# Attention scores in row halves: two heads at once on TensorE, in a kernel of pooled attention followed by a gated two-layer product

## The chip, the cores and the metric

The kernel runs on one core of one Trainium2 chip. The metric is the device time of one execution in microseconds (us); 1000 ns are 1 us. All comparisons of times below use runs of the fast state. Even at full clock two executions of one kernel can differ by over a microsecond (the kernel before took from 305.03 to 306.49 us within one set of rounds, both with a clock of 1.0), so wherever a few hundred nanoseconds matter I read them from the profile, not from the difference of two times.

## The reference, cut to what matters

Eight batches of eight heads, 576 queries, head width 64. Keys and values are first averaged over groups of eight rows, so each head has only 72 keys. Then follow plain attention, and on its output a product, `h * cos(h)`, and a second product.

```python
k_p = k.reshape(B, H, Sp, pool, D).mean(axis=3)       # Sp = 72
v_p = v.reshape(B, H, Sp, pool, D).mean(axis=3)
scores = scale * np.matmul(q, k_p.transpose(0, 1, 3, 2))
...                                                     # softmax, attn @ v_p
h = x @ w_in                                            # 4608 x 512 by 512 x 2048
g = h * np.cos(h)
return g @ w_out                                        # 2048 x 512
```

## The kernel before

The tokens are worked off in nine tiles of 512. Each tile has an up projection (64 matmuls of 512 columns) and a down projection (64 more). Attention for the batch that comes next is slipped between the down matmuls, at fixed places, so that TensorE never runs dry. PSUM is the memory, divided into banks, into which the matmuls write their results. A "unit" is four heads by 256 queries; the "remainder" is all eight heads by the last 64 queries.

```python
def scores(b, u, pair):                       # pair: two PSUM banks
    (c0, n), (h0, nh) = u
    flat = pair.rearrange("p a n -> p (a n)")
    for i in range(nh):
        pj, hp = divmod(h0 + i, 2)
        g, r = divmod(ROW * pj + ORDER[c0 // 64], 2)
        nc.tensor.matmul(flat[:Sp, i * n:(i + 1) * n]...,
                         lhsT=kz[b % 2][:, 2 * (h0 + i) + r, 0:Sp],     # 128 rows, one half zero
                         rhs=att["qT", b][:, g:g + n // 64, hp * 64:hp * 64 + 64])
    ...                                       # one exponential on ScalarE for the unit
...
# places in a tile's down projection: (before which down matmul, what)
fill = [(1, scores of the remainder), (12, its values)]
fill[1:1] = [(5, S_(0, 0))]                   # S_(unit, bank pair): scores; V_: values
fill += [(15, S_(1, 2)), (18, V_(0, 0)), (25, S_(2, 2)), (28, V_(1, 1)), (35, S_(3, 2)), (38, V_(2, 0)),
         (46, V_(3, 1))]
```

(The first `fill` line is shortened.) A score sums over 64 numbers, half of the array's 128 rows. The transposed queries of a head lie in the upper or the lower 64 rows, depending on `r`. The kernel before always runs all 128 rows and pads the keys with zeros in the half that doesn't count.

The softmax here doesn't subtract the row's maximum and nothing guards it: scores larger than these inputs give would overflow.

Of the kernel before, what the change touches and what calls it, by code (L numbers as in the profile page):

```python
# [10 lines left out]
BF16 = mybir.dt.bfloat16  # L11
ACTF = mybir.ActivationFunctionType
ADD = mybir.AluOpType.add

POOL = 8
# [4 lines left out]
def kernel(  # L20
# [9 lines left out]
    nc = tc.nc  # L30
    B, H, S, D = q.shape
    Sp = S // POOL
# [3 lines left out]
    scale = 1.0 / math.sqrt(D)  # L36
# [17 lines left out]
    wpool = ctx.enter_context(tc.tile_pool(name="wpool", bufs=1))  # L54
# [9 lines left out]
    g_sb = wpool.tile([128, FFCH, TILE], BF16, name="g_sb")  # L64

    SpA = -(-Sp // 16) * 16
    kz = [wpool.tile([128, 2 * H, SpA], BF16, name=f"kz{i}") for i in range(2)]

    kpz = [wpool.tile([SpA, H, 4, D], BF16, name=f"kpz{i}") for i in range(2)]

    vz = [wpool.tile([Sp, KCH, 4, D], BF16, name=f"vz{i}") for i in range(2)]

# [6 lines left out]
    staged = {}  # L79

    def even_view(src, b, j0=0, j1=KCH):
        return src[b, 2 * j0:2 * j1].rearrange("(j a) (p t) d -> (a p) j (t d)", a=2, t=ROW)

    def load_even(dst, b, src, j0=0, j1=KCH):
        nc.gpsimd.dma_start(out=dst[:, j0:j1].rearrange("p j t d -> p j (t d)"), in_=even_view(src, b, j0, j1))  # L85
# [37 lines left out]
    att = {}  # L123
    half = (slice(0, 64), slice(64, 128))

    def v_part(b):
        return vz[b % 2][:, :, 0:4:3, :]

    def put_kz(b, ps, pj0, pj1, copy):
        dst = kz[b % 2].rearrange("p (j a r) n -> p j a r n", a=2, r=2)  # L130
        for a in range(2):
            for r in range(2):
                copy(out=dst[half[r], pj0:pj1, a, r, 0:Sp], in_=ps[half[a]])

    def pool_add(b, which):

        st = staged.pop((which, b))
        x = st[:, 0]
        s = st[:, 1].rearrange("p h t d -> p (h t d)").bitcast(FP32).rearrange(
            "p (h t d) -> p h t d", h=H, t=POOL // 2)  # L140
        add = nc.gpsimd.tensor_tensor
        add(out=s, in0=x[:, :, 0:4, :], in1=x[:, :, 4:8, :], op=ADD)  # L142
        add(out=s[:, :, 0:2, :], in0=s[:, :, 0:2, :], in1=s[:, :, 2:4, :], op=ADD)  # L143
        if which == "k":
            for slot in (0, 3):
                add(out=kpz[b % 2][:Sp, :, slot, :], in0=s[:, :, 0, :], in1=s[:, :, 1, :], op=ADD)  # L146
        else:
            s = s.rearrange("p (j a) t d -> p j a t d", a=2)
            add(out=v_part(b), in0=s[..., 0, :], in1=s[..., 1, :], op=ADD)

    def pool_k_mm(b, bank, pj0, pj1):

        kb = staged["k", b]
        ps = bank[:, 0:(pj1 - pj0) * Sp].rearrange("p (j n) -> p j n", n=Sp)
        for pj in range(pj0, pj1):
            for t in range(ROW):
                for rows in half:
                    nc.tensor.matmul(ps[rows, pj - pj0, :], lhsT=kb[rows, pj, t, :], rhs=groups[rows, t, :],
                                     start=(t == 0), stop=(t == ROW - 1))
        return lambda copy: put_kz(b, ps, pj0, pj1, copy)  # L160

    def pool_v_mm(b, pair):
        vb = staged["v", b]
# [5 lines left out]
                              in_=pair[:Sp, :, 0:KCH * D].rearrange("p a (j d) -> p a j d", j=KCH))  # L169

    def k_transpose(b):
        nc.sync.dma_start_transpose(out=kz[b % 2], in_=kpz[b % 2].rearrange("p h s d -> p (h s d)"))


    QB = KCH * ROW // 2
# [11 lines left out]
    def q_transpose_mm(b, bank, g0, g1):  # L187
# [5 lines left out]
            nc.tensor.matmul(ps[:, g - g0, :], q_flat(b)[:, g * 128:(g + 1) * 128], identity, is_transpose=True)  # L193
        return lambda copy: copy(out=att["qT", b][:, g0:g1, :], in_=ps)  # L194

    def scores(b, u, pair):
        (c0, n), (h0, nh) = u
        flat = pair.rearrange("p a n -> p (a n)")
        for i in range(nh):
            pj, hp = divmod(h0 + i, 2)  # L200
            g, r = divmod(ROW * pj + ORDER[c0 // 64], 2)
            nc.tensor.matmul(flat[:Sp, i * n:(i + 1) * n].rearrange("p (g n) -> p g n", n=64),  # L202
                             lhsT=kz[b % 2][:, 2 * (h0 + i) + r, 0:Sp],
                             rhs=att["qT", b][:, g:g + n // 64, hp * 64:hp * 64 + 64])
        ex = asb.tile([Sp, 4 * 256], BF16, name="ex", tag="ex", bufs=EX)
        nc.scalar.activation(out=ex[:, 0:nh * n], in_=flat[:Sp, 0:nh * n], func=ACTF.Exp, scale=scale / POOL)  # L206
        att["ex", b, u] = ex

    def x_out(b, u, rows):
        (c0, n), (h0, nh) = u  # L210
        return xT[rows, h0 // 2:(h0 + nh) // 2, b * S + c0:b * S + c0 + n]

    def cols(x, u):
        n = u[0][1]
        return x[:, 0:n * u[1][1] // 2].rearrange("p (j n) -> p j n", n=n)

    def inverse_tile(w):
        lnc = asb.tile([128, 512], FP32, name="lnc", tag="lnc", bufs=1)
        inv = asb.tile([128, 512], FP32, name="inv", tag="inv", bufs=3)
        return lnc[:, 0:w], inv[:, 0:w]  # L220

    def values(b, u, pair, later=None):

        (c0, n), (h0, nh) = u
        ex = att.pop(("ex", b, u))
        for i in range(nh):
            pj, hp = divmod(h0 + i, 2)
            nc.tensor.matmul(pair[:, hp, (i // 2) * n:(i // 2 + 1) * n],  # L228
                             lhsT=vz[b % 2][:, pj, 2 * hp:2 * hp + 2, :].rearrange("p a d -> p (a d)"),
                             rhs=ex[:, i * n:(i + 1) * n])  # L230
        w = nh * n // 2
        lnc, inv = inverse_tile(w)
        for hp in range(2):
            nc.scalar.activation(out=lnc[half[1 - hp]], in_=pair[half[1 - hp], hp, 0:w], func=ACTF.Ln)  # L234
        nc.scalar.activation(out=inv, in_=lnc, func=ACTF.Exp, scale=-1.0)  # L235

        def mul():
            for hp in range(2):
                nc.vector.tensor_mul(out=x_out(b, u, half[hp]), in0=cols(pair[half[hp], hp, :], u),  # L239
                                     in1=cols(inv[half[1 - hp]], u))  # L240

        if later is None:
            mul()
        else:
            later.append(mul)

    def sums_first(b, u, cs):

        (c0, n), (h0, nh) = u
        ex = att["ex", b, u]  # L250
        for i in range(nh):
            hp = i % 2
            nc.tensor.matmul(cs[hp * 64:hp * 64 + 64, (i // 2) * n:(i // 2 + 1) * n], lhsT=ones[:Sp, :],
                             rhs=ex[:, i * n:(i + 1) * n])
        w = nh * n // 2
        lnc, inv = inverse_tile(w)
        nc.scalar.activation(out=lnc, in_=cs[:, 0:w], func=ACTF.Ln)
        nc.scalar.activation(out=inv, in_=lnc, func=ACTF.Exp, scale=-1.0)
        att["inv", b, u] = inv

    def values_then(b, u, ao):

        (c0, n), (h0, nh) = u
        ex = att.pop(("ex", b, u))
        for i in range(nh):
            pj, hp = divmod(h0 + i, 2)
            nc.tensor.matmul(ao[hp * 64:hp * 64 + 64, (i // 2) * n:(i // 2 + 1) * n],
                             lhsT=vz[b % 2][:, pj, 3 * hp, :], rhs=ex[:, i * n:(i + 1) * n])
        nc.vector.tensor_mul(out=x_out(b, u, slice(0, 128)), in0=cols(ao, u), in1=cols(att.pop(("inv", b, u)), u))

    def exp_tables():
        nc.scalar.preload_act_table_set("natural_log_exp_and_others")  # L272
# [49 lines left out]
    warm = consts.tile([128, 512], BF16, name="warm")  # L322
    nc.vector.memset(warm, 1.0)
    exp_tables()
    nc.vector.memset(kz[0], 0.0)

    kv_even_tiles(0)
    q_tile(0)
# [1 line left out]
    nc.sync.dma_start(out=k_first.rearrange("p (j n) -> p j n", j=2), in_=even_view(k, 0, 0, 2))  # L330
    nc.scalar.copy(out=staged["k", 0][:, 0:2].rearrange("p j t d -> p (j t d)"), in_=k_first)
    load_even(staged["q", 0], 0, q, 0, 2)

    row_of = consts.tile([128, ROW], FP32, name="row_of")
    for rows in half:
# [2 lines left out]
    first_of = consts.tile([128, Sp], FP32, name="first_of")  # L338
    nc.gpsimd.iota(first_of, pattern=[[POOL, Sp]], base=0, channel_multiplier=0,
                   allow_small_or_imprecise_dtypes=True)  # L340
    load_even(staged["k", 0], 0, k, 2, 4)
    identity = consts.tile([128, 128], BF16, name="identity")
    make_identity(nc, identity)
    load_even(staged["q", 0], 0, q, 2, 4)
    load_even(staged["v", 0], 0, v)
    dist = consts.tile([128, ROW, Sp], FP32, name="dist")
    sign = consts.tile([128, ROW, Sp], FP32, name="sign")
    groups = consts.tile([128, ROW, Sp], BF16, name="groups")
# [1 line left out]
                            in1=first_of.unsqueeze(1).to_broadcast([128, ROW, Sp]), op=mybir.AluOpType.subtract)  # L350
# [6 lines left out]
    gate = consts.tile([1, 1], BF16, name="gate")  # L357
# [11 lines left out]
    load_w_out(0)  # L369
    load_even(staged["v", 1], 1, v)  # L370
    for i in range(2):
        nc.gpsimd.memset(kpz[i], 0.0)  # L372
    for cg in range(1, 4):
        load_w_out(cg)

# [22 lines left out]
    sums_first(0, us[1], obanks[1])  # L398
    scores(0, us[2], banks[0])
    scores(0, us[3], banks[2])  # L400
    nc.vector.memset(kz[1], 0.0)
    nc.vector.memset(vz[1], float(POOL))
    pool_v_mm(0, banks[1])
    sums_first(0, us[2], obanks[0])
# [9 lines left out]
    for t in range(NT):  # L414
        b = t + 1
# [29 lines left out]
        def V_(n, bank, wait=None):  # L445
            return lambda: values(b, us[n], banks[bank], wait)
# [25 lines left out]
            sin_tables()  # L472
        if 0 < t and b + 1 < B:

            nc.gpsimd.tensor_copy(out=gate, in_=kz[b % 2][0:1, 0, 0:1])  # L475
        if b + 1 < B:
            load_kv(b + 1, "k", k)
            load_q(b + 1)
# [32 lines left out]
```

## Time and profile before

| | before |
|---|---|
| time, median of all 6 runs beside the change | 305.52 us (305.22 to 306.61) |
| span in the profile | 303.6 us |
| TensorE busy | 97% |
| one steady tile (start of an up projection to the next) | 31.65 us |

In the views PE stands for TensorE's matmuls and PEld for its weight loads, ACT for ScalarE, DVE for VectorE, POOL for GpSimd. The chain in order of time (start, length, what) goes on after the score unit at 68.89 us with seven down matmuls:

```profile
69.32 1.51 PE obank L297 x7
```

The groups of instructions split by shape say (line, engine, operation, names, shapes, count; then busy us and mean ns of one; then idle time of that engine just before, and what ended it):

```profile
L202 PE MATMUL bank<-qT,kz 128*72 128x256 bf16 x128 | 19.2, 273 | 0.3 <-ACT qT L194 0.2
L202 PE MATMUL bank<-qT,kz 128*72 128x64 bf16 x64 | 3.5, 198 | 0.0
...
L297 PEld LDWEIGHTS <-g_sb 128*128 128x128 bf16 x560 | 53.8, 98 | 50.5 <-issue 0.2
```

The mean of 273 ns is the length of one record, not its cost: successive ones start 109 ns apart. And the weight loads run ahead. The load for the first score of the unit at 68.72 us starts at 68.51:

```profile
68.51 0.11 PEld L202 LDWEIGHTS <-kz 128*72 128x72 bf16 x1
```

The idle time of the weight loads before the down matmuls is 50.5 us, some 90 ns a load. Only 0.2 us of it is put down to "issue", because the view names a cause for the longer gaps alone.

### The profile page before, as it was taken

Reading aid. Unit: us, or ns where it says so; the run is one execution under the profiler, and the core shown is the slowest. Engines: PE = TensorE matmul, PEld = TensorE weight load, DVE = VectorE, ACT = ScalarE, POOL = GpSimd, SP = SyncE. Lnnn points to the kernel's source line nnn. Section 1 sums busy time; section 2 is a strip of 40 time slices with the busy share of each in tenths; the row PEclk is TensorE's granted clock in tenths of the full one; section 3 lists DMA queues with packets and bytes.
Section 4 is the critical chain, followed back from the end, with each engine's and each line's share of the span. In section 5 each row is a group of like instructions: output and inputs, shape, how many; then the busy total and the mean of one; then the engine's idle time right before and its main releaser. Section 6 shows DMA issues by size and latency. Waiting matters only on the chain.

```text
span 303.6 us, 4590 instructions
## 1 busy us (share of the span) xinstructions
PE 295.3 (97%) x1798; PEld 152.5 (50%) x1798; DVE 173.3 (57%) x213; ACT 206.6 (68%) x255; POOL 131.8 (43%) x92
## 2 busy tenths in 40 slices
PE   6899999999999999999999999999999999999995
PEld 2645654446544554455445544565455544444444
DVE  7558546574566555745575566637574657425712
ACT  3886897469956995689668966797569946605500
POOL 8573017985963596339823990399100000000000
PEclk9999999999999999999999999999999999999999
DMA  7999999649455934694379527871911120031032
GB/s 145 193 207 206 209 203 196 147 82 177 101 129 103 171 74 100 123 170 86 85 146 162 105 48 178 125 145 35 167 26 36 37 69 0 21 85 35 0 71 71
DMA packets 47846, 33.90 MB, mean 112 GB/s; under 512 B 25936, under 2 KB 43088, under 8 KB 47824
## 3 DMA queue, kind: packets, MB, share of 16 engines
q0 software_dynamic: 19744, 18.07, 38.0%
q1 hardware_dynamic: 27920, 15.41, 22.0%
q8 instruction: 14, 0.23, 0.3%
q10 hardware_dynamic: 160, 0.13, 0.2%
q14 instruction: 8, 0.07, 0.1%
HBM read 36.70 MB, written 9.44 MB: 152 GB/s over the span
## 4 chain that ended last, share of the span: by engine, by line
PE 85%; DMA 9%; POOL 3%; ACT 1%; issue 0%; DVE 0%; POOLq 0%; ACTq 0%
PE obank L297 38%; PE bank L284 36%; DMA w_out_sb<-in_moe_w_out_dram 6%; PE bank L228 5%; PE bank L202 4%; DMA w_in_sb<-in_moe_w_in_dram 3%; PE bank L315 1%; POOL kpz L372 1%; POOL kv_st L85 1%; POOL q_b L85 1%; ACT L272 0%; ACT cos L291 0%; POOL identity masks.py:199 0%; ACT ex L206 0%; DVE o_sb L303 0%
## 5 line engine op out<-in xcount | busy, mean ns | idle before, releaser
L297 PE MATMUL obank<-w_out_sb,g_sb 128*128 128x512 bf16 x560 | 134.2, 379 | 0.1
L284 PE MATMUL bank<-xT,w_in_sb 128*128 128x512 bf16 x576 | 126.3, 379 | 0.0
L291 ACT ACTIVATE cos<-bank,half_pi 128x1024 f32<-128x1024 f32 x72 | 80.1, 1114 | 67.3 <-PE bank L284 67.3
L294 DVE TENSOR_TENSOR g_sb<-bank,cos 128x1024 bf16<-128x1024 f32 x72 | 88.1, 1225 | 50.1 <-ACT cos L291 50.1
L284 PEld LDWEIGHTS <-w_in_sb 128*128 128x128 bf16 x576 | 56.1, 98 | 67.3 <-issue 0.4
L297 PEld LDWEIGHTS <-g_sb 128*128 128x128 bf16 x560 | 53.8, 98 | 50.5 <-issue 0.2
L239 DVE TENSOR_TENSOR xT<-bank,inv 64x512 bf16<-64x512 f32 (+1 forms) x72 | 45.3, 629 | 49.5 <-ACT inv L235 49.0
L142 POOL TENSOR_TENSOR kv_st<-kv_st 72x2048 f32<-72x2048 bf16 x12 | 48.8, 4064 | 34.7 <-DMA kv_st<-in_k_dram 34.7
L234 ACT ACTIVATE lnc<-bank 64x512 f32<-64x512 f32 (+1 forms) x72 | 39.2, 544 | 4.7 <-PE bank L228 3.1
L206 ACT ACTIVATE ex<-bank 72x1024 bf16<-72x1024 f32 (+1 forms) x40 | 36.1, 925 | 0.7 <-PE bank L202 0.6
L303 DVE COPY o_sb<-obank 128x512 f32<-128x512 f32 x35 | 23.6, 690 | 16.7 <-PE obank L297 16.1
L143 POOL TENSOR_TENSOR kv_st<-kv_st 72x1024 f32<-72x1024 f32 x12 | 28.2, 2349 | 1.0
L202 PE MATMUL bank<-qT,kz 128*72 128x256 bf16 (+1 forms) x192 | 22.7, 248 | 0.3 <-ACT qT L194 0.2
L202 PEld LDWEIGHTS <-kz 128*72 128x72 bf16 x192 | 17.5, 114 | 9.1 <-issue 0.6
L235 ACT ACTIVATE inv<-lnc 128x512 f32<-128x512 f32 (+1 forms) x36 | 21.0, 583 | 1.1
L228 PE MATMUL bank<-ex,vz 72*128 72x256 bf16 (+1 forms) x176 | 20.1, 243 | 0.3 <-ACT ex L206 0.2
L228 PEld LDWEIGHTS <-vz 72*128 72x128 bf16 x176 | 13.7, 97 | 9.9 <-issue 0.7
L146 POOL TENSOR_TENSOR kpz<-kv_st 72x512 bf16<-72x512 f32 x12 | 15.0, 1267 | 0.5
L272 ACT ACT_TABLE_LOAD x9 | 11.5, 1283 | 0.9 <-PEq L495 0.7
L475 POOL COPY gate<-kz 1x1 bf16<-1x1 bf16 x5 | 0.9, 180 | 25.9 <-DMA kz<-kpz 25.9
L275 ACT ACT_TABLE_LOAD x9 | 11.5, 1283 | 0.2
L85 POOL DMA_DIRECT2D q_b<-in_q_dram x10 | 7.7, 773 | 2.9 <-DMA w_in_sb<-in_moe_w_in_dram 1.4
(57 smaller groups left out, 91.1 us busy)
## 6 DMA issues: line engine op xcount, KB each, us to landing
out_dram<-o_sb SPq DMA_DIRECT2D x70, 128.0 KB, 2.4
kv_st<-in_v_dram POOLq DMA_DIRECT2D x8, 576.0 KB, 12.8
kv_st<-in_k_dram POOLq DMA_DIRECT2D x7, 576.0 KB, 7.7
q_b<-in_q_dram POOLq DMA_DIRECT2D x6, 576.0 KB, 9.8
w_in_sb<-in_moe_w_in_dram POOLq DMA_DIRECT2D x4, 512.0 KB, 13.0
w_out_sb<-in_moe_w_out_dram POOLq DMA_DIRECT2D x4, 512.0 KB, 18.6
q_b<-in_q_dram POOLq DMA_DIRECT2D x4, 288.0 KB, 11.5
g_sb<-in_k_dram SPq DMA_DIRECT2D x1, 576.0 KB, 3.4
```

Of the source, the lines that this page charges most:

```text
L142: add(out=s, in0=x[:, :, 0:4, :], in1=x[:, :, 4:8, :], op=ADD)
L143: add(out=s[:, :, 0:2, :], in0=s[:, :, 0:2, :], in1=s[:, :, 2:4, :], op=ADD)
L202: nc.tensor.matmul(flat[:Sp, i * n:(i + 1) * n].rearrange("p (g n) -> p g n", n=64), lhsT=kz[b % 2][:, 2 * (h0 + i) + r, 0:Sp], rhs=att["q ...
L206: nc.scalar.activation(out=ex[:, 0:nh * n], in_=flat[:Sp, 0:nh * n], func=ACTF.Exp, scale=scale / POOL)
L228: nc.tensor.matmul(pair[:, hp, (i // 2) * n:(i // 2 + 1) * n], lhsT=vz[b % 2][:, pj, 2 * hp:2 * hp + 2, :].rearrange("p a d -> p (a d)"), ...
L234: nc.scalar.activation(out=lnc[half[1 - hp]], in_=pair[half[1 - hp], hp, 0:w], func=ACTF.Ln)
L239: nc.vector.tensor_mul(out=x_out(b, u, half[hp]), in0=cols(pair[half[hp], hp, :], u), in1=cols(inv[half[1 - hp]], u))
L284: nc.tensor.matmul(h[:, j, :], lhsT=w_in_sb[fc // 4][:, ki, (fc % 4) * 128:(fc % 4 + 1) * 128], rhs=xT[:, ki, t * TILE:(t + 1) * TILE], st ...
L291: nc.scalar.activation(out=cos, in_=h, func=ACTF.Sin, bias=half_pi[:, :1])
L294: nc.vector.tensor_mul(out=g_sb[:, 2 * fp:2 * fp + 2, :], in0=h, in1=cos)
L297: nc.tensor.matmul(o, lhsT=g_sb[:, fc, ms * 128:(ms + 1) * 128], rhs=w_out_sb[fc // 4][:, fc % 4, :], start=(fc == 0), stop=(fc == FFCH - 1))
L303: nc.vector.tensor_copy(out=o[:, 0:n], in_=ps)
```

## The change

The intent: two heads whose queries lie in different row halves run at the same time, each in its half of the array and with a PSUM bank of its own. The keys are kept once in each half, without zeros. On the side, the loads of batch 0 are issued sooner, and the identity for the transposes is built behind them.

```diff
-    kz = [wpool.tile([128, 2 * H, SpA], BF16, name=f"kz{i}") for i in range(2)]
-    kpz = [wpool.tile([SpA, H, 4, D], BF16, name=f"kpz{i}") for i in range(2)]
+    kk = [wpool.tile([128, H, SpA], BF16, name=f"kk{i}") for i in range(2)]
+    kp2 = [wpool.tile([SpA, H, 2, D], BF16, name=f"kp2{i}") for i in range(2)]
...
+        for i in [i + 2 * a for k in range(0, nh, 4) for i in (k, k + 1) for a in range(2)]:
+            bank, c = divmod(ex_col(u, i), nh * n // 2)
...
-                             lhsT=kz[b % 2][:, 2 * (h0 + i) + r, 0:Sp],
-                             rhs=att["qT", b][:, g:g + n // 64, hp * 64:hp * 64 + 64])
+                             lhsT=kk[b % 2][half[r], h0 + i, 0:Sp],
+                             rhs=att["qT", b][half[r], g:g + n // 64, hp * 64:hp * 64 + 64])
...
     load_even(staged["q", 0], 0, q, 0, 2)
+    load_even(staged["k", 0], 0, k, 2, 4)
...                                            (index ramps)
-    load_even(staged["k", 0], 0, k, 2, 4)
+    load_even(staged["q", 0], 0, q, 2, 4)
+    load_even(staged["v", 0], 0, v)
     identity = consts.tile([128, 128], BF16, name="identity")
     make_identity(nc, identity)
-    load_even(staged["q", 0], 0, q, 2, 4)
-    load_even(staged["v", 0], 0, v)
```

(Cut: the zeroing of `kz`, the copies into `kk`, and the index `ex_col`, by which the values find a head's columns in their new order. Heads 0, 2, 1, 3 of a unit now follow each other.)

More of the change, by code (lines that the diff above doesn't have):

```diff
@@ L127, in v_part, with put_kk @@
         return vz[b % 2][:, :, 0:4:3, :]
-    def put_kz(b, ps, pj0, pj1, copy):
-        dst = kz[b % 2].rearrange("p (j a r) n -> p j a r n", a=2, r=2)
+    def put_kk(b, ps, pj0, pj1, copy):
+        dst = kk[b % 2].rearrange("p (j a) n -> p j a n", a=2)
         for a in range(2):
             for r in range(2):
-                copy(out=dst[half[r], pj0:pj1, a, r, 0:Sp], in_=ps[half[a]])
+                copy(out=dst[half[r], pj0:pj1, a, 0:Sp], in_=ps[half[a]])
     def pool_add(b, which):
@@ L144, in pool_add @@
         if which == "k":
-            for slot in (0, 3):
-                add(out=kpz[b % 2][:Sp, :, slot, :], in0=s[:, :, 0, :], in1=s[:, :, 1, :], op=ADD)
+            for slot in range(2):
+                add(out=kp2[b % 2][:Sp, :, slot, :], in0=s[:, :, 0, :], in1=s[:, :, 1, :], op=ADD)
         else:
@@ L159, in pool_k_mm @@
                                      start=(t == 0), stop=(t == ROW - 1))
-        return lambda copy: put_kz(b, ps, pj0, pj1, copy)
+        return lambda copy: put_kk(b, ps, pj0, pj1, copy)
     def pool_v_mm(b, pair):
@@ L171, in k_transpose @@
     def k_transpose(b):
-        nc.sync.dma_start_transpose(out=kz[b % 2], in_=kpz[b % 2].rearrange("p h s d -> p (h s d)"))
+        nc.sync.dma_start_transpose(out=kk[b % 2], in_=kp2[b % 2].rearrange("p h s d -> p (h s d)"))
     QB = KCH * ROW // 2
@@ L194, in q_transpose_mm, with ex_col @@
         return lambda copy: copy(out=att["qT", b][:, g0:g1, :], in_=ps)
+    def ex_col(u, i):
+        (c0, n), (h0, nh) = u
+        return (i // 2 % 2 * (nh // 2) + i // 4 * 2 + i % 2) * n
     def scores(b, u, pair):
         (c0, n), (h0, nh) = u
-        flat = pair.rearrange("p a n -> p (a n)")
-        for i in range(nh):
+        for i in [i + 2 * a for k in range(0, nh, 4) for i in (k, k + 1) for a in range(2)]:
+            bank, c = divmod(ex_col(u, i), nh * n // 2)
             pj, hp = divmod(h0 + i, 2)
             g, r = divmod(ROW * pj + ORDER[c0 // 64], 2)
-            nc.tensor.matmul(flat[:Sp, i * n:(i + 1) * n].rearrange("p (g n) -> p g n", n=64),
-                             lhsT=kz[b % 2][:, 2 * (h0 + i) + r, 0:Sp],
-                             rhs=att["qT", b][:, g:g + n // 64, hp * 64:hp * 64 + 64])
+            nc.tensor.matmul(pair[:Sp, bank, c:c + n].rearrange("p (g n) -> p g n", n=64),
+                             lhsT=kk[b % 2][half[r], h0 + i, 0:Sp],
+                             rhs=att["qT", b][half[r], g:g + n // 64, hp * 64:hp * 64 + 64])
         ex = asb.tile([Sp, 4 * 256], BF16, name="ex", tag="ex", bufs=EX)
-        nc.scalar.activation(out=ex[:, 0:nh * n], in_=flat[:Sp, 0:nh * n], func=ACTF.Exp, scale=scale / POOL)
+        nc.scalar.activation(out=ex[:, 0:nh * n].rearrange("p (a n) -> p a n", a=2), in_=pair[:Sp, :, 0:nh * n // 2],
+                             func=ACTF.Exp, scale=scale / POOL)
         att["ex", b, u] = ex
@@ L229, in values @@
                              lhsT=vz[b % 2][:, pj, 2 * hp:2 * hp + 2, :].rearrange("p a d -> p (a d)"),
-                             rhs=ex[:, i * n:(i + 1) * n])
+                             rhs=ex[:, ex_col(u, i):ex_col(u, i) + n])
         w = nh * n // 2
@@ L253, in sums_first @@
             nc.tensor.matmul(cs[hp * 64:hp * 64 + 64, (i // 2) * n:(i // 2 + 1) * n], lhsT=ones[:Sp, :],
-                             rhs=ex[:, i * n:(i + 1) * n])
+                             rhs=ex[:, ex_col(u, i):ex_col(u, i) + n])
         w = nh * n // 2
@@ L267, in values_then @@
             nc.tensor.matmul(ao[hp * 64:hp * 64 + 64, (i // 2) * n:(i // 2 + 1) * n],
-                             lhsT=vz[b % 2][:, pj, 3 * hp, :], rhs=ex[:, i * n:(i + 1) * n])
+                             lhsT=vz[b % 2][:, pj, 3 * hp, :], rhs=ex[:, ex_col(u, i):ex_col(u, i) + n])
         nc.vector.tensor_mul(out=x_out(b, u, slice(0, 128)), in0=cols(ao, u), in1=cols(att.pop(("inv", b, u)), u))
@@ L324 @@
     exp_tables()
-    nc.vector.memset(kz[0], 0.0)
     kv_even_tiles(0)
@@ L371 @@
     for i in range(2):
-        nc.gpsimd.memset(kpz[i], 0.0)
+        nc.gpsimd.memset(kp2[i], 0.0)
     for cg in range(1, 4):
@@ L400 @@
     scores(0, us[3], banks[2])
-    nc.vector.memset(kz[1], 0.0)
     nc.vector.memset(vz[1], float(POOL))
@@ L473 @@
         if 0 < t and b + 1 < B:
-            nc.gpsimd.tensor_copy(out=gate, in_=kz[b % 2][0:1, 0, 0:1])
+            nc.gpsimd.tensor_copy(out=gate, in_=kk[b % 2][0:1, 0, 0:1])
         if b + 1 < B:
```

## The prediction

> **What bounds the kernel now.** I read the engine shares first, then the chain of waits in order of time, then the groups split by shape, and last narrow windows of the timeline around single matmuls.
>
> The first view is the page's busy times and its chain. TensorE is busy for 97% of the span and carries 85% of the chain; no other engine comes near.
>
> ```profile
> PE 295.3 (97%) x1798; PEld 152.5 (50%) x1798; DVE 173.3 (57%) x213; ACT 206.6 (68%) x255; POOL 131.8 (43%) x92
> ...
> PE 85%; DMA 9%; POOL 3%; ACT 1%; issue 0%; DVE 0%; POOLq 0%; ACTq 0%
> ```
>
> The chain in order of time (start, length, what) says where this holds. Up to 38.10 us it is the queue of loads, of which the second quarter of the down weights lands last; TensorE stands in it without a break for six tiles, and one detour through ScalarE comes in the eighth:
>
> ```profile
> 6.14 10.26 DMA w_in_sb<-in_moe_w_in_dram
> ...
> 20.92 17.18 DMA w_out_sb<-in_moe_w_out_dram
> 38.10 0.04 issue
> 38.14 0.81 PE obank L297 x3
> 38.95 0.44 PE bank L202 x4
> ...
> 67.53 0.22 PE obank L297
> 67.75 0.27 PE bank L202 x8
> 68.02 0.86 PE obank L297 x4
> 68.89 0.44 PE bank L202 x4
> ...
> 257.45 1.11 ACT cos L291
> 258.56 0.02 issue
> 258.58 1.28 ACT L272
> 259.87 0.01 ACTq L234
> 259.87 0.01 issue
> 259.88 0.60 ACT ex L206
> 260.48 0.04 issue
> 260.52 0.39 PE bank L228 x8
> ```
>
> So between 48.5 and 257.4 us every nanosecond added to or taken from TensorE's stream shows in the end time; outside that stretch there are waits that swallow it. The score matmuls are line 202. A unit of four heads by 256 queries costs 0.44 us of stream, and the remainder unit (eight heads by 64 queries) 0.27 us. There are 32 units and 8 remainders (128 matmuls and 64 in the groups split by shape), so the scores hold 32 x 0.437 + 8 x 0.273 = 16.2 us of TensorE. If two heads at a time were free of cost, at most half of it, some 8 us or 2.6%, could go.
>
> **What the Trainium skill says.** Three places bear on this. "TensorE: Matmul & The Clock Gate", section "Part 3: Packing small matmuls", says that matmuls in different row groups run at the same time and start about 4 ns apart. The trace agrees: pooling V already works in 64-row halves with a bank each (line 166), its two matmuls start 3 to 4 ns apart, and a pair of 256 columns follows the next at 106 to 109 ns, where line 202 takes 109 ns for a single one. "TensorEngine Tiling (Array Packing)", section "Gotcha 1: PSUM Pressure", says that different row tiles cannot use one PSUM bank at once; the change gives each half its own bank, as line 166 does. The same page, section "Key Properties", says "Mode switching requires drain: Changing tiling mode (not just tile) drains the TensorE", without a figure. This kernel shows the figure, and it decides the case.
>
> **What a switch costs.** Two narrow windows of the timeline, each cut so that it starts with the last matmul before a switch (start, length, line, shapes, count):
>
> ```profile
> 13.55 0.27 PE L202 MATMUL bank<-qT,kz 128*72 128x256 bf16 x1
> 13.75 0.30 PE L166 MATMUL bank<-kv_st,groups 64*72 64x256 bf16 x2
> ...
> 37.40 0.27 PE L166 MATMUL bank<-kv_st,groups 64*72 64x256 bf16 x1
> 37.61 0.26 PE L228 MATMUL bank<-ex,vz 72*128 72x64 bf16 x3
> ```
>
> In both, start to start is 0.20 us (203 and 202 ns in the records), where two matmuls of one mode would be 109 ns apart. Going into row halves costs 94 ns, coming out 93 ns; nothing else was being waited for, and the weight loads, which normally run ahead, start only at the end of the gap too. The up projection into pooling K (26.08 to 26.39, 309 instead of 216 ns) and back (27.55 to 27.68, 127 instead of about 32) gives +93 and +95. Two small costs go with it: the second pair after a switch comes after 136 ns instead of 109, and the second matmul after coming back is 11 ns late (227 instead of 216).
>
> **The change part by part.**
>
> A unit of four heads in the down projection. Before: 4 x 109 = 437 ns. After: in 94, first pair to second pair 136, its second half 4, then last score to next down matmul 202 (109 of stream and 93 out), 11 for the late second one: 447 ns. The halved streaming is spent on the two switches: +10 ns a unit.
>
> A remainder unit, eight matmuls of 64 columns. Before 8 x 35 = 273 ns with the edges. These were bound not by columns but by the 72-column weight loads, at 35 ns each. Line 158 (pooling K, 72 columns in both halves) shows pairs of such size: 53 ns from first to second pair, then 33. After: in 94, then 53 + 35 + 35 for four pairs, 3 for the second half of the last, 35 of stream, 93 out, 11 late: 359 ns, +86 ns.
>
> In the six tiles where TensorE is never idle, each has one remainder and four units: 86 + 4 x 10 = 126 ns, six times is 0.76 us. These lie fully on the path.
>
> The eighth tile: its remainder is followed by a wait of 407 ns before the values at 260.52 (ScalarE ends the last cosine, loads its table, does the exponential). 86 ns more TensorE work before it disappears in it: 0.
>
> The first tile: before the values of its remainder are followed by the down matmuls of the second weight quarter, TensorE is 292 ns late because those weights land at 38.098; later a wait of 200 ns at 47.5 stands before values, behind a ScalarE that is nearly always busy. The 86 and 4 x 10 ns fall into these: 0 to 0.04.
>
> Batch 0, before 17.6 us: two runs of eight scores become four pairs each, 0.87 to about 0.45 us of stream. The switch out of the second run also disappears, since pooling V is in the same mode. But ScalarE is busy back to back here from 9.41 to 19.67 us, and the scores wait for transposed queries which ScalarE copies at 12.39 to 12.96. I expect 0.2 to 0.3 us sooner for TensorE at 17.6 us, and this ends in a longer wait for the weights at 38.1: 0.
>
> The zeroing of the padded keys on VectorE (2 x 0.59 us) was beside other work: 0. The zeroed GpSimd tile becomes half as large, 2 x 1.8 us to about 2 x 0.9 us. After it comes the issue of the down weights at 20.92; they land 17.2 us later, because the queue in front of them is full. Each load lands 2.5 to 2.8 us behind its predecessor. An earlier issue brings nothing. The transposes of keys by DMA halve too (3.6 us each, issued about ten microseconds before use): 0.
>
> The moved loads. The pieces of K, Q and V of batch 0 are issued 0.6 to 1.2 us sooner, since the identity (0.22 + 0.89 us) goes behind them; the weights keep their place. Before, the second and third pieces landed 1.53 and 1.68 us after their predecessor, while an equal piece in the full queue took 1.43 (24.34 to 25.77). If this slack of 0.10 + 0.25 us closes, everything behind lands up to 0.35 us sooner, the down weights included: 0 to -0.35, I take -0.15. On the other side the index ramps on GpSimd come about 0.8 us later, so the pooling matrix is ready at about 5.8 us instead of 5.1 and the first pooling matmul starts 0.4 us later. What follows waits for the Q load at 7.6 us, so 0 to 0.2 us is left of that, and the 9.4 to 19.7 stretch decides it: 0 to +0.1.
>
> Sum: +0.76 + 0.02 - 0.15 + 0.03 = +0.66, hence 305.33 + 0.6, about 305.9 us.
>
> **The rivals.** First: the switches are hidden, because weight loads of another row group are pulled ahead. Then 28 units would gain about 0.19 us and the remainders 0.1, about 6 us: 299 us, faster by 2%. For it: half of the score streaming really goes. Against it: the trace holds this very pair of neighbours, full rows into halves and back, at 94 and 93 ns each time. Second: a switch costs more between score and down matmuls than where I read it, for instance because the down weights then can't be loaded ahead of a 512-column matmul. At 50 ns more for each of 2 x 35 switches it is +3.5 us, 309. Against: the switch out of the up projection is the same size. Third: the start becomes the bound, that is, the late pooling matrix delays the first exponential by up to 0.4 us and ScalarE hands this on to 20 us. It would be hidden by the 292 ns wait at 38.1 except for some 0.1 us: 306.0. Fourth: the order of loads gains the whole 0.35 us and nothing else changes: 305.7.
>
> **Range and chances.** The on-path sum is two numbers of nearly equal size subtracted, so it is small whichever way the remainder comes out: 304.8 to 307.0 should hold it 8 times in 10; the upper side is longer because one of the three runs before was 306.61. Faster by over 2% needs the first rival in full (4%), slower by over 2% a switch of twice the size (2%).
>
> **What would show it.** In the changed profile a score unit in the steady tiles should show two pairs, each 3 to 4 ns apart, with 0.31 us from the down matmul before to the first score (216 + 94) and 0.20 us from the last score to the next down matmul; unit and remainder should hold 0.44 and 0.36 us of stream and a steady tile 31.77 us instead of 31.65. The load of the second down weights should land between 37.7 and 38.1, with TensorE waiting for it. I am wrong if the gaps at the switches are much under 90 ns (then faster), or if the stretch from 48.5 to 257.4 us changes by more than 1.5 us either way.

## The result, and the profile after

| | before | after |
|---|---|---|
| time, median of 6 | 305.52 us | 306.32 us (306.01 to 306.97) |
| span in the profile | 303.6 us | 304.2 us |
| start of the second tile | 53.56 us | 53.48 us |
| one steady tile | 31.647 us | 31.768 us |
| eighth tile | 28.54 us | 28.54 us |
| from the start of the ninth tile to the end | 31.58 us | 31.58 us |

The ratio is 1.0024, with a 95% interval of 1.0006 to 1.0043. Ratios and intervals here are worked out from the fast runs of the same rounds, so not quite the ratio of the medians. The kernel is a little slower, and well within 2%. The tile rows come from the starts of the matmuls in the trace. The six steady tiles took 189.88 us before and 190.61 after: +0.73 us. The start gave back 0.08, and the two last tiles nothing: 0.65 us in sum, the difference of the unrounded spans (303.56 and 304.21).

The page's busy times and chain after:

```profile
PE 295.6 (97%) x1798; PEld 140.2 (46%) x1798; DVE 172.0 (57%) x211; ACT 206.4 (68%) x255; POOL 129.5 (43%) x92
...
PE 84%; DMA 11%; POOL 2%; ACT 1%; issue 0%; DVE 0%; POOLq 0%; ACTq 0%
```

TensorE is as busy as before, though its scores were to take half the time. The groups split by shape say why this line cannot show it:

```profile
L303 PEld LDWEIGHTS <-g_sb 128*128 128x128 bf16 x560 | 51.3, 98 | 56.2 <-issue 6.0
...
L207 PE MATMUL bank<-qT,kk 64*72 64x256 bf16 x128 | 13.0, 282 | 1.3 <-DVE qT L193 0.6 <-ACT qT L193 0.5
L207 PEld LDWEIGHTS <-kk 64*72 64x72 bf16 x192 | 6.6, 109 | 17.2 <-issue 16.8 <-DVE qT L193 0.4
L207 PE MATMUL bank<-qT,kk 64*72 64x64 bf16 x64 | 2.6, 201 | 0.0
```

The scores' busy time fell from 19.2 to 13.0 us and from 3.5 to 2.6, a handsome 7.1 us. What it was paid with stands in the other column: the weight loads' idle time rose from 9.1 to 17.2 us before the scores and from 50.5 to 56.2 before the down matmuls. (The "issue" part rose more, from 0.6 to 16.8 and from 0.2 to 6.0, but only because gaps that were too short to be named are now long enough.) In that time no weights are loaded ahead:

```profile
68.83 0.11 PEld L207 LDWEIGHTS <-kk 64*72 64x72 bf16 x2 [0.42 <-issue]
```

The first load of the new mode starts 308 ns after the start of the last down matmul (68.52 us), so 92 ns after the 216 ns of that one's stream. In the kernel before it started within 2 ns of the same matmul's start.

The chain in order of time, at the same place of the second tile as before:

```profile
40.66 0.04 issue
40.70 0.59 PE obank L303 x2
...
68.90 0.34 PE bank L207 x4
69.24 1.62 PE obank L303 x7
```

A reader who compares the score line alone sees 0.34 us instead of 0.44 and calls it a gain. But the seven down matmuls after it have grown from 1.51 to 1.62 us. The sum is 1.95 us before and 1.96 after: the chain books the switch back to full rows on the line that follows it. The first rows show the start: TensorE now waits at 40.7 us, for the third quarter of the down weights, where it waited at 38.1 for the second.

Two narrow windows of the timeline, each from the last matmul before a switch:

```profile
68.52 0.38 PE L303 MATMUL obank<-w_out_sb,g_sb 128*128 128x512 bf16 x1
68.83 0.30 PE L207 MATMUL bank<-qT,kk 64*72 64x256 bf16 x2
...
68.97 0.27 PE L207 MATMUL bank<-qT,kk 64*72 64x256 bf16 x1
69.17 0.39 PE L303 MATMUL obank<-w_out_sb,g_sb 128*128 128x512 bf16 x1
```

From start to start it is 309 ns into the halves, of which 216 are the stream of a down matmul, so 93 are lost; coming out it is 202, of which 109 are stream, so 93 again. The two scores of a pair start 4 ns apart, the second pair 137 ns after the first, and the second down matmul after the visit is 10 to 11 ns late.

### The profile page after: what moved, and what is told of

Same layout as the page of the kernel before. It is cut to its first block, busy times and chain, and to the rows that moved or that the text cites. A ratio compares the mean times of both kernels' runs of the same rounds, so it can differ in the third digit from the quotient of the medians.

```text
span 304.2 us, 4587 instructions
## 1 busy us (share of the span) xinstructions
PE 295.6 (97%) x1798; PEld 140.2 (46%) x1798; DVE 172.0 (57%) x211; ACT 206.4 (68%) x255; POOL 129.5 (43%) x92
## 4 chain that ended last, share of the span: by engine, by line
PE 84%; DMA 11%; POOL 2%; ACT 1%; issue 0%; DVE 0%; POOLq 0%; ACTq 0%
PE obank L303 39%; PE bank L290 36%; DMA w_out_sb<-in_moe_w_out_dram 6%; DMA w_in_sb<-in_moe_w_in_dram 5%; PE bank L234 5%; PE bank L207 3%; PE bank L321 1%; POOL q_b L84 1%; POOL kv_st L84 0%; POOL w_in_sb L112 0%; ACT L278 0%; ACT cos L297 0%; ACT ex L211 0%; DVE o_sb L309 0%; POOL row_of L342 0%
## 5 line engine op out<-in xcount | busy, mean ns | idle before, releaser
L303 PEld LDWEIGHTS <-g_sb 128*128 128x128 bf16 x560 | 51.3, 98 | 56.2 <-issue 6.0
L240 ACT ACTIVATE lnc<-bank 64x512 f32<-64x512 f32 (+1 forms) x72 | 39.1, 544 | 5.9 <-PE bank L234 4.7
L207 PE MATMUL bank<-qT,kk 64*72 64x256 bf16 (+1 forms) x192 | 15.6, 255 | 1.3 <-DVE qT L193 0.6
L145 POOL TENSOR_TENSOR kp<-kv_st 72x512 bf16<-72x512 f32 x12 | 14.9, 1263 | 0.5
L207 PEld LDWEIGHTS <-kk 64*72 64x72 bf16 x192 | 6.6, 109 | 17.2 <-issue 16.8
L479 POOL COPY gate<-kk 1x1 bf16<-1x1 bf16 x5 | 0.9, 180 | 25.9 <-DMA kk<-kp 25.9
```

What stands on the lines that cost most here:

```text
L207: nc.tensor.matmul(pair[:Sp, bank, c:c + n].rearrange("p (g n) -> p g n", n=64), lhsT=kk[b % 2][half[r], h0 + i, 0:Sp], rhs=att["qT", b][h ...
L240: nc.scalar.activation(out=lnc[half[1 - hp]], in_=pair[half[1 - hp], hp, 0:w], func=ACTF.Ln)
L303: nc.tensor.matmul(o, lhsT=g_sb[:, fc, ms * 128:(ms + 1) * 128], rhs=w_out_sb[fc // 4][:, fc % 4, :], start=(fc == 0), stop=(fc == FFCH - 1))
```

## The experiments

Theory: a visit to the row halves (one group of scores between down matmuls) has a fixed price, whatever is done in it. A unit of two pairs just about pays it and a remainder doesn't, so six steady tiles lose 0.73 us. Rivals: the reordered start costs the time; the pairs are concurrent only in appearance; the wait lies elsewhere, in the schedule or on ScalarE. Twelve kernels ran, all with correct results. "Tile" is the mean of the six steady tiles in the run's profile. Kernels that ran together share the runs of the kernel before: its median was 305.46 us beside the first four, 305.64 beside the next four, 305.41 beside the next three and 305.46 beside the last.

**The scores alone** (`scores_only`): the change without its moved loads.

```diff
     load_even(staged["q", 0], 0, q, 0, 2)
-    load_even(staged["k", 0], 0, k, 2, 4)
...
+    load_even(staged["k", 0], 0, k, 2, 4)
+    identity = consts.tile([128, 128], BF16, name="identity")
+    make_identity(nc, identity)
     load_even(staged["q", 0], 0, q, 2, 4)
     load_even(staged["v", 0], 0, v)
-    identity = consts.tile([128, 128], BF16, name="identity")
-    make_identity(nc, identity)
```

> The change without its moved loads and identity. Theory (fixed cost per visit to the row halves): a steady tile takes 31.77 us as in the changed kernel against 31.65 before, so +0.7 us in six tiles; the second quarter of the down weights lands at 38.1 us as before (38.098), not at 37.5, and TensorE waits for that one and not for the third. Time about 306.3 us, 0.7 to 0.8 over before. Rival (the start, reordered, is what costs): a steady tile may be as it is, but the time is that of before, 305.5, because the reordering is missing.

Measured: tile 31.769 us; median 306.41 us, ratio 1.0047 (1.0005 to 1.0089). Two of its six runs had a lowered clock (0.982) and over 310 us; one of them widens the interval. The four at full clock took 305.94 to 306.53. The second quarter of the down weights landed at 38.18 us, as before. The loss in the tiles is the same as in the whole change, so it comes from the scores.

**The loads alone** (`loads_only`): the kernel before with the moves of the diff just shown, the other way round.

> The kernel before with only the loads and the identity moved as in the change. Theory: steady tiles unchanged at 31.65 us; the down weights' second quarter lands about 0.5 us sooner (37.5 to 37.7), the third quarter decides instead, and no more than 0.1 us of it reaches the end: 305.4 us, ratio 0.999 to 1.000. Rival (the start costs): 306.2, ratio 1.002 or more.

Measured: tile 31.646 us; median 305.78 us, ratio 1.0008 (0.9992 to 1.0024). The tiles are as expected and the rival falls. But the second quarter landed at 38.27 us, not sooner: that part of the expectation missed. In the runs below that share this order of loads it landed between 37.3 and 39.1 us. So neither my -0.15 us for the start nor the 0.08 us that the profiled run showed there can be put down to the moved loads.

**Units in halves, remainder in full rows** (`units_halves`), and **the reverse** (`rest_halves`). Both keep the padded keys of before; one line differs between them.

```diff
+    def halves(u):
+        return u[0][1] == 256            # rest_halves: == 64
...
+            rows = half[r] if in_halves else slice(0, 128)
-                             lhsT=kz[b % 2][:, 2 * (h0 + i) + r, 0:Sp],
-                             rhs=att["qT", b][:, g:g + n // 64, hp * 64:hp * 64 + 64])
+                             lhsT=kz[b % 2][rows, 2 * (h0 + i) + r, 0:Sp],
+                             rhs=att["qT", b][rows, g:g + n // 64, hp * 64:hp * 64 + 64])
```

> The kernel before with its padded keys and its loads; only the units of four heads by 256 queries read the keys in row halves, in pairs with a bank each; the remainder unit stays in full rows. Theory: per unit +10 ns, so a steady tile is 31.65 + 0.04 = 31.69 us and the time 305.5 + 0.24 = 305.8. Rival (switches cost the remainder and the units alike because the down weights are loaded late): the tile comes to 31.75 or more.

> The complement: only the remainder unit of eight heads by 64 queries in row halves, the four units in full rows as before. Theory: +0.09 us a tile, 31.73 to 31.74 us, and 305.5 + 0.5 = 306.0; this and the run with only the units add up to the whole loss of the steady tiles (0.04 + 0.09 = 0.12 to 0.13 us a tile). Rival as in the run with only the units: the remainder accounts for a fifth (one visit in five), 31.67.

Measured: 31.680 us a tile with the units alone, +0.033 or 8 ns a unit; 31.733 with the remainder alone, +0.086. Together 0.119, against 0.121 in the whole change. So one visit in five, the remainder's, makes 70% of the loss, because it has the least streaming to save. The times themselves say little here: in the first, half of the runs had a clock of 0.983 and over 309 us (median 307.81, ratio 1.0056), and its three runs at full clock took 305.57 to 306.33; in the second two runs had 0.989 and 0.993 (median 306.14, ratio 1.0048).

**More visits, the same matmuls** (`split`): one down matmul between the two pairs of each unit.

```diff
-            fill[1:1] = [(5, S_(0, 0))]
-            fill += [(15, S_(1, 2)), (18, V_(0, 0)), (25, S_(2, 2)), (28, V_(1, 1)), (35, S_(3, 2)), (38, V_(2, 0)),
-                     (46, V_(3, 1))]
+            fill[1:1] = [(5, half_S(0, 0, 0)), (6, half_S(0, 0, 1))]
+            fill += [(15, half_S(1, 2, 0)), (16, half_S(1, 2, 1)), (18, V_(0, 0)),
+                     (25, half_S(2, 2, 0)), (26, half_S(2, 2, 1)), (28, V_(1, 1)),
+                     (35, half_S(3, 2, 0)), (36, half_S(3, 2, 1)), (38, V_(2, 0)), (46, V_(3, 1))]
```

> The changed kernel with one down matmul put between the two pairs of each unit in the six steady tiles: four visits more per tile, the same matmuls. Theory: a visit more costs 94 in + 93 out + 11 late, and saves the 27 ns by which a second pair after a switch is late: +171 ns a unit, 24 units, +4.1 us; tile 31.77 + 0.68 = 32.45 us, time 310.4. Rival (the pairs only look concurrent in the profile and the matmuls themselves take the time; switches are cheap): within 1 us of the changed kernel, 306 to 307.

Measured: tile 32.677 us, +0.909 over the changed kernel, or 227 ns for each of the four visits more; median 311.54 us, ratio 1.0207 (1.0148 to 1.0265), so slower, though whether by 2% stays unclear. One of its four runs had a clock of 0.984 and took 315.25 us; the three at full clock took 310.88 to 311.63. The price of a visit is real. I had the price itself too low, at 171. The timeline of this run shows where:

```profile
67.98 0.38 PE L306 MATMUL obank<-w_out_sb,g_sb 128*128 128x512 bf16 x1
68.29 0.30 PE L208 MATMUL bank<-qT,kk 64*72 64x256 bf16 x2
68.52 0.39 PE L306 MATMUL obank<-w_out_sb,g_sb 128*128 128x512 bf16 x1
68.84 0.30 PE L208 MATMUL bank<-qT,kk 64*72 64x256 bf16 x2
```

A lone pair is followed by the next down matmul after 229 ns, not 202. The first pair after a switch is itself some 28 ns late (its records last 297 ns instead of 269), and whoever comes next waits for that, be it a second pair or a down matmul. I had booked it as a cost of the second pair. So a visit that begins with a pair of 256 columns costs 94 + 28 + 93 + 11 = 226 ns. For one that begins with the remainder's 64 columns the trace shows 21 in place of the 28 (records of 217 ns instead of 196).

**Plain order of heads** (`no_pairs`): heads 0, 1, 2, 3, whose halves are 0, 0, 1, 1 (or the reverse), so that neighbours share a half.

```diff
-        for i in [i + 2 * a for k in range(0, nh, 4) for i in (k, k + 1) for a in range(2)]:
+        for i in range(nh):
```

> The changed kernel with its heads in plain order, so that two successive matmuls use the same row half and only the middle two of four overlap: same switches, less overlap. Theory: three slots of 109 ns instead of two per unit, five of 35 instead of four in the remainder: +0.109 x 4 + 0.035 = +0.47 us a tile, 32.24 us, time 306.3 + 2.8 = 309.1. Rival (pairing brings nothing): unchanged at 31.77 us.

Measured: tile 31.784 us, only 0.016 more than with pairs; median 306.76 us, ratio 1.0030 (0.9983 to 1.0077). My expectation was wrong, and the time is that of its rival; but the rival's reason doesn't hold either, since the scores still overlap two by two, as two narrow windows show:

```profile
69.13 0.30 PE L207 MATMUL bank<-qT,kk 64*72 64x256 bf16 x2
...
69.27 0.28 PE L207 MATMUL bank<-qT,kk 64*72 64x256 bf16 x2
69.48 0.39 PE L303 MATMUL obank<-w_out_sb,g_sb 128*128 128x512 bf16 x1
```

In the program the first two matmuls are of the same half, and the built program keeps that order (a fresh build of this kernel lists the halves as 0, 0, 1, 1 or 1, 1, 0, 0). Strictly in order they would need three slots. In the trace it is two slots, 137 ns apart, with the two matmuls of each 6 to 7 ns apart (3 to 4 with pairs). The trace doesn't say which matmul a record is, so this is inferred: TensorE started the first matmul of the other half before the second one of the same half. The order of heads in the change is therefore hardly needed.

**One visit less** (`join_one`): the remainder's scores move behind the fifth down matmul, directly in front of unit 0. And its **control** (`join_one_full`): the same move in the kernel before.

```diff
+            fill[0] = (5, fill[0][1])
             fill[1:1] = [(5, S_(0, 0))]
```

> The changed kernel with the remainder's scores moved behind the fifth down matmul, directly before unit 0, in the six steady tiles: four visits instead of five, all else as it was. Theory: 94 + 93 + 11 and some 20 ns of the late second pair go with each visit: -0.2 to -0.22 us a tile, 31.55 to 31.57 us, below the 31.65 of before; time 306.3 - 1.25 = 305.0, just faster than before (ratio 0.998). Rival (a wait takes its place, ScalarE's exponential of the remainder comes later): 31.77 us or more.

> Control: the kernel before, scores in full rows, with the same move of the remainder to unit 0. Theory: no switches, so nothing to save: tile 31.65 us, time 305.5, ratio 1.000. Rival (it is the place of the remainder and not the switch that the joined run gains by): the same -0.2 us a tile, 31.44.

Measured: 31.637 us with halves (median 305.31, ratio 0.9982, 0.9948 to 1.0017) and 31.651 in the control. The control's steady tiles ran at full clock; by its time (306.02, ratio 1.0013) nothing moved. So the gain is one of switches and not of place. It was 0.131 us, though, and not 0.2. A narrow window shows what took the rest:

```profile
71.32 0.38 PE L303 MATMUL obank<-w_out_sb,g_sb 128*128 128x512 bf16 x1
71.63 0.19 PE L234 MATMUL bank<-ex,vz 72*128 72x64 bf16 x1
```

Start to start it is 310 ns where a down matmul needs 216. Neither line is in row halves: this is no switch but a wait of 94 ns, which the changed kernel doesn't have before these values. ScalarE's exponential of the remainder ends at 71.58 us, just before they start: TensorE had become faster than it.

**The same, the values one place later** (`join_one_later`):

```diff
-            fill[0] = (5, fill[0][1])
-            fill[1:1] = [(5, S_(0, 0))]
+            fill = [(5, fill[0][1]), (5, S_(0, 0)), (13, fill[1][1])]
```

> As the run with the remainder's scores joined to unit 0, with the remainder's values one down matmul later (thirteenth instead of twelfth). In the first joined run the tile came to 31.637 instead of 31.55, and its values started 94 ns late each tile. Theory (a wait for the exponential of the remainder, which one down matmul of 216 ns covers): 31.54 us a tile, the whole 226 ns of one visit saved, 305.0 us or a little less. Rival (a joined visit itself saves only 130 ns): 31.64 us as in the first joined run.

Measured: tile 31.547 us, 0.221 below the changed kernel; median 304.64 us, ratio 0.9980 (0.9967 to 0.9993). The whole price of a visit came back.

**Three visits** (`join_two`) and its **control** in full rows (`join_two_full`):

```diff
-            fill[1:1] = [(5, S_(0, 0))]
-            fill += [(15, S_(1, 2)), (18, V_(0, 0)), (25, S_(2, 2)), (28, V_(1, 1)), (35, S_(3, 2)), (38, V_(2, 0)),
-                     (46, V_(3, 1))]
+            fill = [(6, fill[0][1]), (6, S_(0, 0)), (13, fill[1][1]), (19, S_(1, 2)), (19, S_(2, 0)),
+                    (26, V_(0, 1)), (33, S_(3, 2)), (36, V_(1, 0)), (43, V_(2, 1)), (46, V_(3, 2))]
```

> The changed kernel with three visits to the row halves per steady tile instead of five: remainder and unit 0 together after the sixth down matmul, units 1 and 2 together after the nineteenth, unit 3 alone after the thirty-third; the values moved to fit the banks. Taking the lone-pair figure of the run with split units, a visit costs 94 + 28 + 93 + 11 = 226 ns. Theory: 31.77 - 2 x 0.226 = 31.32 us a tile, 0.33 below the kernel before; time 306.3 - 2.7 = 303.6, ratio to before 0.993 to 0.995. Rival (ScalarE, which is nearly always busy in the down projection, or a bank held by the values becomes the wait): waits of TensorE in the tile, 31.5 us or more, no gain over before.

> Control for the run with three visits: the kernel before, full rows, with the same places of scores and values. Theory: no switches to save, so 31.65 us a tile or, where the new places bring waits, a little more; 305.5. Rival (the gain of the run with three visits is one of schedule): 31.3 here too.

Measured: 31.32 us in four of the tiles and 31.38 in two (the control has the same 0.06 in the same two, so that is the schedule's); median 303.56 us, ratio 0.9942 (0.9928 to 0.9956). The control: 31.65 in four and 31.71 in two, 305.52 us, ratio 1.0003 (0.9989 to 1.0017). The sum with 226 ns a visit holds to the hundredth.

**Two visits** (`two_visits`), the version that beats both kernels:

```diff
+            fill = [(10, fill[0][1]), (10, S_(0, 0)), (10, S_(1, 1)),
+                    (14, lambda: values(t, REST, banks[2])), (22, S_(2, 0)), (22, S_(3, 1)),
+                    (27, V_(0, 2)), (32, V_(1, 0)), (36, V_(2, 1)), (46, V_(3, 2))]
```

> The last step of the same kind: two visits per steady tile. The remainder and units 0 and 1 together after the tenth down matmul (ScalarE begins its exponentials only about then), units 2 and 3 together after the twenty-second, the values moved to fit the banks. Theory: 31.32 - 0.226 = 31.09 us a tile, six tiles 1.36 us less than the run with three visits: 302.2, ratio to before about 0.990. Rival (the schedule is now ScalarE's or the banks': the values come later and the next tile waits for them): waits of TensorE show in the tile, 31.3 us or more, 303.5 or more.

Measured: tile 31.108 us; median 302.14 us, ratio 0.9890 (0.9869 to 0.9911). It is 1.1% faster than before; by the medians 3.3 us faster than before and 4.2 faster than the change as given (that one ran in other rounds). No control in full rows was run for these places. That the schedule by itself brings nothing was shown for three visits only; here the sum of the prices speaks for it, 31.77 - 3 x 0.226 = 31.09 us against 31.108 measured. Its chain in order of time:

```profile
67.61 2.16 PE obank L303 x10
69.77 0.71 PE bank L207 x16
70.48 0.97 PE obank L303 x4
...
73.41 0.56 PE bank L207 x8
73.97 1.19 PE obank L303 x5
```

Twenty-four scores now stand in two groups. Sixteen, the remainder and two units, take 0.71 us; in five visits the remainder (0.26) and two units (0.34 each) took 0.94, by the chain's own way of booking.

## Why the prediction was right or wrong

The time, 306.32 us, lies in the range, and 0.4 us above the stated 305.9. Of this, 0.1 is a slip: 305.33 + 0.66 is 305.99. By the prediction's own steps:

- **What bounds the kernel.** Right: the whole change of the steady tiles came through to the end, +0.73 us of tiles in a span that grew by 0.65.
- **The price of a switch.** Right: 94 in and 93 out were read from pooling V and the up projection, and 93 and 93 were measured at the scores. The second rival, 50 ns more per switch, fell; so did the first, weights loaded ahead through a switch. The readings were thinner than they sound. The only down matmul that ran into halves before the change (36.10 us) shows 403 ns from start to start, because the matmul after it also waited for VectorE until 36.46; only the weight load there, 307 ns after the down matmul, told that the price was the same. And the pairs of pooling V start 3 to 4 ns apart in the first visit (13.75 us) only; in the second (36.50) they are mostly 32 to 35 ns apart. Reducing visits at equal work shows the price as directly as adding them does.
- **The unit.** Mechanism and size right: +10 ns predicted, +8 measured. **The remainder**: +86 predicted and measured. That its matmuls were bound by the loads of 72 columns is only half shown: matmuls of as many columns at line 228, with other weights, follow each other after 29 ns and not 35, so columns alone do not set it; that the loads do was not tested. A steady tile: 31.77 us predicted, 31.768 measured.
- **The eighth tile.** Right: 28.54 us in both; its wait before the values shrank from 407 to 319 ns, by about the 86 of the remainder.
- **The first tile and the start.** This step failed in its detail. The second weight quarter landed at 37.51 us, 0.59 sooner and below my 37.7 to 38.1, and TensorE did not wait for it. It waited 0.41 us for the third quarter, which landed at 40.66 as before (40.64). The slack behind "I take -0.15" did not close: the second and third pieces landed 1.83 and 1.73 us after their predecessors (before: 1.53 and 1.68), and most of the 0.59 us was there already in the first Q load, which landed at 7.08 us instead of 7.59 although it was issued at 1.27 in both. The run with the moved loads alone brought no gain. That the start changed the time so little is luck: in the fast profiles the second tile starts anywhere from 52.94 to 54.55 us. Why the third quarter came 3.15 us after the second in this run, where it is 2.5 to 2.9 in all others, is open. The medians differ by 0.80 us and the profiled spans by 0.65; the two profiled runs themselves took 305.34 and 306.01 us, 0.67 apart, so the rest is the spread of the runs.
- **Found only by experiment.** The prediction counts 136 ns "to the second pair" as the property of a second pair. The sum for a unit came out right that way, but the cost belongs to the visit, as the lone pairs showed.

## What to carry to other kernels

Before packing small matmuls into row halves, read from a trace what a switch of mode costs and compare it with the streaming saved in one visit, not in the whole kernel: here a visit of two pairs saved 218 ns (4 x 109 less 2 x 109) and cost 226. If the two are close, collect the packed work into fewer, longer visits, and move what depends on it so that no wait takes the place of the switch. When reading the result, add up the lines on both sides of the changed one, since the chain books the way back on the line that follows.

## What the Trainium skill lacked or had wrong

- "TensorEngine Tiling (Array Packing)", section "Key Properties", says that a change of mode drains TensorE and gives no figure. The runs show 93 to 94 ns into row halves and 93 out of them, 28 ns for a late first pair of 256 columns (21 for the remainder's 64) and 10 to 11 for the second matmul after coming back: 226 ns a visit by the sum, 227 by the run with four more visits a tile, 221 by the first one less.
- "TensorE: Matmul & The Clock Gate", section "Part 3: Packing small matmuls", calls matmuls strictly in order, with no reordering. With heads in plain order (halves 0, 0, 1, 1) four scores ran in two slots and not in three; the tile took 31.784 us, against 31.768 with explicit pairs. Order seems to hold within a row group only; as told above, this is inferred, as the trace doesn't name the matmul of a record.
- The same section, under "The mechanism", lets weight loads for a row group that doesn't conflict, or for the background buffer, be pulled ahead of matmuls, and doesn't say what becomes of this at a change of mode. The runs show none pulled ahead across one: the first load of the scores starts 308 ns after the down matmul before it, where in the kernel before it started within 2 ns, and the idle time before the scores' loads rose from 9.1 to 17.2 us.
